# Attention groups with filler: nine score and maximum pairs instead of eight

## The chip, the cores and the metric

The kernel runs on one core of one Trainium2 chip. The metric is the device time of one execution in microseconds (us). The kernel before took a median of 1838.41 us over 3 runs (1837.89 to 1838.9).

The names of the engines are those of the profile: PE is TensorE (PEld its weight loads), DVE is VectorE, ACT is ScalarE, POOL is GpSimd, SP is SyncE.

## What is computed

One transformer block with adaptive normalization, 2048 tokens of width 512, 32 heads of 16, and a gated feed-forward layer of width 1792. Cut to what matters:

```python
mod = silu(c) @ w_mod                                # six vectors sa, ca, ga, sb, cb, gb
h = layernorm(x) * (1 + ca) + sa
q, k, v = (h @ wqkv), cut into 32 heads of 16
p = softmax(q k^T / 4);  o = p v                     # 2048 x 2048 for each head
x = x + ga * (o @ wo)
h = layernorm(x) * (1 + cb) + sb
x = x + gb * ((silu(h @ w_gate) * (h @ w_up)) @ w_down)
```

## The kernel before

**Units and steps.** The queries are cut into 4 chunks of 512, the heads into 8 groups of 4. A chunk and a head group make a unit; there are 32 units. A unit has 16 steps (one for each 128 keys), so there are 512 steps of 4 heads, and 2048 *pairs*. A pair is one score matmul (`score`, L568: keys by queries, whose exponential ACT takes at L570 out of the bank into a tile `pt`, which 13 buffers hold in turn) and one maximum matmul (`max_one`, L521: queries by keys in the other half of the array's rows, whose row maximum DVE takes at L523). The maxima belong to a unit that comes about 20 steps later, whose scores then have their row maximum taken off before the exponential. When a unit's maxima are complete, DVE reduces them (L545), ACT and DVE turn them into rows, and SP sends these to `qop`.

**Value products.** For each step, `pv_step` multiplies the exponentials by the values in two halves of 256 queries (L583: 4 heads side by side in the array's columns, each matmul twice in the trace). One bank, number 7, holds the sum over a unit's 16 steps. After the last step ACT copies the bank to the tile `o` (L587), and the next unit starts in the same bank. `pvs` issues the halves that are due: the first argument bounds their number, and a step may be taken when `4 * step + 8 <= done`, where `done` counts the pairs issued so far.

**Plain and filled stretches.** In a *plain* stretch (`plain`) PE does three pairs, then one or two halves, and so on; scores go round three banks, maxima round four. While the attention of chunk 1, 2 and 3 goes on, the output projection and the feed-forward layer of the chunk before are worked in as *filler*, in *groups* (`filled`): eight pairs with twelve slots of filler between them, then what is queued in `hook` (DVE's work on a finished filler job), then up to six halves, a *burst*. A slot is two matmuls of 64 rows into the banks 3 and 6 (L781). In a group scores go round two banks (4, 5) and maxima round three (0, 1, 2). A tuple says how many slots follow each pair: `TWO` for the output projection and for `gate_up` (24 slots, two groups), `DOWN` for `down` (12 slots, one group). `gate_up` ends with a tanh on ACT (L835) and two DVE operations that empty the banks (L839, L841); `down` ends with two DVE additions (L855), and in its middle ACT reads both banks (L878) before the second six slots may write them.

**What sets the order.** Everything is written out by hand: each engine's queue holds its instructions in the order of the Python calls. A chunk's filler starts at a step of the table `STARTS`: 32 pairs of output projection, plain stretches of `NORM` = 9 and `WIN` = 3 steps, for the last one also `REST` = 24 steps, then the feed-forward jobs, with one plain stretch of 3 steps before the last two `down` jobs. What is left before the next start is plain. `close_unit` sets the steps at which a finished unit's output is scaled and stored, and at which the next chunk's tiles are taken and loaded (`begin`, `load_wo`, `load_o`) and split on POOL (`split_o`). The last 20 steps have no maxima; their groups take eight pairs in five banks.

Of the kernel before, what the change touches and what calls it, by code (L numbers as in the profile page):

```python
# [29 lines left out]
NG = H // 4  # L30
NU = NG * NC
NF = F // P
FG = 2
# [10 lines left out]
PTS = 13  # L44
FBANKS = (3, 6)
KEEP = 7
REST = 24
NORM = 9
STARTS = (147, 275, 403)
TWO = (0, 3, 2, 2, 2, 2, 1, 0)  # L50
DOWN = (0, 3, 3, 0, 3, 3, 0, 0)
ALONE = {TWO: (0, 4, 0, 4, 0, 4, 0, 0), DOWN: (0, 6, 0, 0, 0, 6, 0, 0)}


def run(it):
    for _ in it:
        pass


def take(it, k):  # L60
    run(islice(it, k))
# [40 lines left out]
def block_kernel(ctx, tc, x, wqkv, wo, w_gate, w_up, w_down, c, w_mod, out):  # L102
    nc = tc.nc
# [18 lines left out]
    four, bank, single = Turn(0, 1, 2, 3), Turn(4, 5, 6), Turn(7)  # L122
# [231 lines left out]
    bank = Turn(4, 5, 6, 7)  # L354
# [101 lines left out]
    for ci in range(NC - 1):  # L456
# [6 lines left out]
        if ci == 1:  # L463
            bank = Turn(4, 5, 6)
# [30 lines left out]
    n = 16 * NU  # L495
    last = NC - 1
# [93 lines left out]
    def out_a(u, eng):  # L590
        pv.pop(u)
        o = o_.pop(u)
        dn = pf.tile([P, 16], F32, name="dn", tag="dn", bufs=1)
        eng.dma_start(dn, o[16:P:32, :].rearrange("h (b e) -> h b e", e=16))
        return o, dn
# [17 lines left out]
    def at(i, f):  # L613
        due.setdefault(i, []).append(f)
# [257 lines left out]
    chunks = {}  # L872
# [7 lines left out]
    def begin(ci):  # L880
        x2 = pf.tile([P, 4, D], F32, name="x2", tag="x2", bufs=1)
        act = [pf.tile([P, NK, CW], F32R, name=f"act{a}", tag=f"act{a}", bufs=1) for a in range(2)]
        hT = [pf.tile([P, NK, CW], F32R, name=f"act{a}", tag=f"act{a}", bufs=1) for a in range(2)]
        chunks[ci] = ch = Chunk(ci, x2, act, hT)
        ch.load_x2(nc.sync if ci else nc.gpsimd)
# [18 lines left out]
    four, bank = Turn(0, 1, 2, 3, 6, 7), Turn(4, 5)  # L904
# [4 lines left out]
    def close_unit(u, i):  # L909

        if u == NU - 1:
            res[u] = out_a(u, nc.scalar)
            return
        res[u] = out_a(u, nc.sync)
        if u + 3 < NU:
            load_k(u + 3)
            load_q(u + 3)
        i0 = i if u % NG == NG - 1 else i + 3
        at(i0 + 3, lambda: res.__setitem__(u, out_b(u, nc.sync, *res[u])))
        at(i0 + 4, lambda: res.__setitem__(u, out_r(u, nc.sync, *res[u])))  # L920
        at(i0 + 5, lambda: out_c(u, nc.gpsimd, nc.gpsimd, *res.pop(u)))
        if u % NG == NG - 1:
            if u // NG:
                at(i + 4, lambda: begin(u // NG))
                at(i + 5, lambda: chunks[u // NG].load_wo())
            at(i + 7, lambda: chunks[u // NG].load_o(nc.gpsimd))
            at(i + 9, lambda: chunks[u // NG].split_o())

    at(3, lambda: begin(0))
    at(UG - 2, lambda: chunks[0].load_wo())  # L930
# [26 lines left out]
    halves = [(i, half) for i in range(n) for half in range(2)]  # L957
    done, ended, owed = 0, 0, 0
    three = Turn(0, 1, 2)
# [15 lines left out]
    for i in range(-LEAD, -1):  # L975
# [7 lines left out]
        if i == -2:  # L983
            four, work = three, bank
            for k in range(4):
                bank = Turn(7, 3, 6)
                for _ in range(WIN):
                    pair_of()
                bank = work
# [3 lines left out]
        while side:  # L993
            side.pop(0)()

    def pvs(most, by_halves):

        nonlocal owed
        if by_halves:
            most, owed = most + owed, 0  # L1000
        while most and halves and 4 * halves[0][0] + 8 <= done:
            i, half = halves.pop(0)
            pv_step(i, half)
            most -= 1
            if i % 16 == 15 and half:
                close_unit(i // 16, done // 4 - 1)
                if by_halves:
                    break
        if by_halves and most and halves and 4 * halves[0][0] + 8 <= done:
            owed = most  # L1010
# [18 lines left out]
            pvs((HALVES[(w - 2) % 4] if done > 8 else 0) + (w == 4 * steps // WIN - 1), True)  # L1029
            end_steps()  # L1030

    def filled(places, work):

        nonlocal four, bank, beside
        beside = True
        four, bank = three, Turn(4, 5)
        if done >= 4 * n - 4 * (LEAD - 1):
            places, bank = ALONE.get(places, places), Turn(4, 5, 0, 1, 2)
        for r in range(len(places)):
            pair_of()  # L1040
            take(work, places[r])
            if r % 4 == 3:
                end_steps()
        hook()
        pvs(6, False)

    def two_of(u):
        return [kop[u % 3][:, e, :].rearrange("p (k c) -> p k c", k=NK) for e in range(2)]
# [11 lines left out]
    for ci in range(last):  # L1060
        plain(STARTS[ci] - done // 4)
        ch = chunks[ci]
        for t0 in (0, 2):
            work = out_pair(ch, t0, outs, True)
            filled(TWO, work)
            filled(TWO, work)
        side.append(lambda: scaled(ch))
        plain(NORM)
        plain(WIN, [lambda tp, k=k: ch.turned(tp, k) for k in range(NK)])
        if ci == last - 1:  # L1070
            plain(REST)
        for _ in range(len(ch.jobs) - (KEEP if ci == last - 1 else 0)):
            job, args = ch.jobs.pop(0)
            if args == (NF // FG - 1, 0):
                plain(WIN)
            work = job(ch, *args, outs, True)
            for places in (TWO, TWO) if job is gate_up else (DOWN,):
                filled(places, work)
    chunks[last - 1].load_gu(NF - 2)
    filled((0,) * 4, iter(()))  # L1080


    assert done == 4 * n
# [75 lines left out]
```

## Time and profile before

| what | number |
|---|---|
| median of 3 runs | 1838.41 us |
| the profiled execution | 1838.88 us |
| its span, from first to last instruction | 1837.1 us |
| busy: PE, DVE, ACT, POOL | 99%, 83%, 68%, 25% of the span |
| granted TensorE clock | 1.00 in every stretch |
| plain stretch before the filler of chunk 1: 84 pairs | 885.49 to 936.64 |
| plain stretch before the filler of chunk 2: 84 pairs | 1291.26 to 1342.66 |
| plain stretch `REST`: 96 pairs | 1404.37 to 1463.35 |
| 40 groups of chunk 0's feed-forward jobs: 320 pairs | 592.58 to 864.19 |

The times of the table's last four rows are the starts of the score matmuls with these numbers, counted along the trace. A busy engine is one with an instruction in flight. PE's matmuls overlap in the trace, since they are pipelined; what one costs is read from start to start. The same holds for the exponentials and the maxima: an instruction's duration is longer than the distance to the next one behind it.

### The profile page before, as it was taken

What the parts mean: (1) busy time and instruction counts of PE and PEld (TensorE: products, weight loads), DVE (VectorE), ACT (ScalarE), POOL (GpSimd) and SP (SyncE); (2) the same over time, 40 slices, a digit from 0 to 9 for tenths busy, and PEclk for the clock granted to TensorE, in tenths of its full rate; (3) what the DMA queues carried; (4) which work ended last, traced back from release to release, by engine and by line L of the source; (5) the groups of instructions that cost most, each with busy time, mean ns of one, the idle gap of its engine ahead of it and who ended that gap; (6) DMA issues with size and microseconds to landing.
All of it is one profiled execution on the core that took longest, in us unless ns stands there. A gap on an engine that the chain in (4) does not pass through costs nothing.

```text
span 1837.1 us, 41048 instructions
## 1 busy us (share of the span) xinstructions
PE 1825.5 (99%) x16904; PEld 1198.2 (65%) x16904; DVE 1532.5 (83%) x2578; ACT 1243.7 (68%) x2386; POOL 460.4 (25%) x541
## 2 busy tenths in 40 slices
PE   9999999999999999999999999999999999999999
PEld 7876444444455777776565777776564577777887
DVE  5578999999999888889999888889999988831544
ACT  4223888888877777777878777777878877774211
POOL 3612544565223111111123111111123011130200
PEclk9999999999999999999999999999999999999999
DMA  8884876657845444453544554444643545333642
GB/s 305 286 225 149 183 185 199 168 189 178 209 79 125 102 120 141 118 147 70 149 103 105 134 132 116 123 117 90 158 81 57 111 93 149 138 122 121 271 169 110
DMA packets 80488, 267.63 MB, mean 146 GB/s; under 512 B 19604, under 2 KB 24212, under 8 KB 59620
## 3 DMA queue, kind: packets, MB, share of 16 engines
q1 hardware_dynamic: 61324, 179.71, 33.8%
q0 software_dynamic: 18288, 84.49, 19.3%
q8 instruction: 133, 2.18, 0.5%
q10 hardware_dynamic: 688, 0.80, 0.2%
q14 instruction: 55, 0.45, 0.1%
HBM read 201.85 MB, written 62.13 MB: 144 GB/s over the span
## 4 chain that ended last, share of the span: by engine, by line
PE 96%; DVE 2%; ACT 1%; DMA 1%; SPq 0%; issue 0%; DVEq 0%
PE bank L583 27%; PE bank L781 19%; PE bank L568 18%; PE bank L521 14%; PE bank L791 8%; PE bank L211 7%; DVE mx L523 1%; PE bank L824 1%; DMA wm_ab<-in_w_mod 1%; PE bank L765 0%; DVE stt L807 0%; PE bank L533 0%; PE bank L163 0%; PE bank L534 0%; PE bank L535 0%
## 5 line engine op out<-in xcount | busy, mean ns | idle before, releaser
L523 DVE TENSOR_REDUCE mx<-bank 128x1 f32<-128x512 f32 x2048 | 1276.0, 681 | 108.5 <-PE bank L521 66.2
L568 PE MATMUL bank<-qop,kop 50*128 50x512 f32 x2048 | 730.2, 425 | 1.0 <-ACT pt__16517 L570 0.2
L521 PE MATMUL bank<-kop,qop 48*128 48x512 f32 x2048 | 726.6, 425 | 2.9 <-DVE mx L523 2.6
L568 PEld LDWEIGHTS bank<-qop,kop 50*128 50x128 f32 x2048 | 342.6, 184 | 169.9 <-issue 55.6
L521 PEld LDWEIGHTS bank<-kop,qop 48*128 48x128 f32 x2048 | 343.5, 184 | 113.9 <-DVE mx L523 67.7
L781 PE MATMUL bank<-act,wgu 64*128 64x512 f32 x1872 | 300.9, 392 | 0.0
L781 PEld LDWEIGHTS bank<-act,wgu 64*128 64x128 f32 x1872 | 196.1, 187 | 24.7 <-issue 0.2
L610 POOL TENSOR_TENSOR on<-o,rb 128x512 f32<-128x512 f32 x31 | 39.8, 1284 | 498.1 <-DMA rb<-d_dr 363.6
L781 PE MATMUL bank<-wd,mid 64*128 64x512 f32 x912 | 134.0, 397 | 0.0
L843 POOL CAST mid<-m 128x512 fp32r<-128x512 f32 x40 | 24.3, 608 | 379.3 <-DVE m L841 176.5
L781 PEld LDWEIGHTS bank<-wd,mid 64*128 64x128 f32 x912 | 88.0, 185 | 15.9 <-ACT first L878 3.2
L211 PE MATMUL bank<-hT,wqs 128*128 128x512 f32 x384 | 94.3, 397 | 0.4 <-DVE wqs L351 0.4
L839 DVE SCALAR_TENSOR_TENSOR q<-th,bank 128x512 f32<-128x512 f32 x56 | 38.2, 682 | 54.4 <-ACT th L835 54.4
L211 PEld LDWEIGHTS bank<-hT,wqs 128*128 128x128 f32 x384 | 70.7, 188 | 18.8 <-issue 2.9
L835 ACT ACTIVATE th<-bank 128x512 f32<-128x512 f32 x56 | 33.3, 594 | 58.1 <-PE bank L791 58.1
L855 DVE TENSOR_TENSOR x<-bank,x 128x512 f32<-128x512 f32 x84 | 53.9, 685 | 18.3 <-PE bank L781 16.8
L841 DVE TENSOR_TENSOR m<-bank,q 128x512 f32<-128x512 f32 x56 | 38.7, 691 | 21.7 <-PE bank L791 19.7
L844 POOL TENSOR_TENSOR mid<-m,mid 128x512 fp32r<-128x512 f32 x40 | 51.5, 1287 | 3.3
L791 PE MATMUL bank<-wd,mid 128*128 128x512 f32 x216 | 51.4, 393 | 0.0
L211 PE MATMUL bank<-wqs,hT 128*128 128x512 f32 x192 | 48.0, 398 | 0.0
L781 PE MATMUL bank<-wgu,act 64*128 64x512 f32 x288 | 47.8, 394 | 0.1
L791 PEld LDWEIGHTS bank<-wd,mid 128*128 128x128 f32 x216 | 40.3, 188 | 9.1 <-POOL mid L844 0.3
(6298 smaller groups left out, 5133.0 us busy)
## 6 DMA issues: line engine op xcount, KB each, us to landing
wgu<-gu_dr SPq DMA_DIRECT2D x48, 1024.0 KB
wd<-wd_dr SPq DMA_DIRECT2D x28, 1024.0 KB
kop<-kd SPq DMA_DIRECT2D x33, 768.0 KB
kop<-kd POOLq DMA_DIRECT2D x29, 768.0 KB, 8.8
gu_dr<-wgu POOLq DMA_DIRECT2D x14, 1024.0 KB, 13.5
kd<-prt SPq DMA_DIRECT2D x16, 512.0 KB
qd<-prt SPq DMA_DIRECT2D x16, 512.0 KB
kop<-gu_dr SPq DMA_DIRECT2D x8, 1024.0 KB
```

The lines of the kernel that those rows point to most:

```text
L211: nc.tensor.matmul(pt, lhs(a, k), rhs(b, k), start=(n == 0), stop=(n == 3 * nk - 1))
L521: nc.tensor.matmul(pm, qop[u][rows, s, qt * P:(qt + 1) * P], kop[u % 3][rows, s, kc * CW:(kc + 1) * CW], start=True, stop=True)
L523: nc.vector.tensor_reduce(mx[u][:, b, s, qt, kc:kc + 1], pm, op=ALU.max, axis=AX.X)
L568: nc.tensor.matmul(sp, kop[u % 3][rows, h // 2, kt * P:(kt + 1) * P], qop[u][rows, h // 2, :], start=True, stop=True)
L583: nc.tensor.matmul(pv[u][32 * h:32 * h + 32, cols], v_flat[:, e0:e0 + 32], p_[h][:, cols], start=(kt == 0 and half == 0), stop=(kt == 15), ...
L610: mul.tensor_mul(on, o, rb)
L781: nc.tensor.matmul(outs[e], lhs(e, a, k)[rows], rhs(b, k)[rows], start=(ph == 0 and j == 0), stop=(j == z and (ph == 1 or trade is not None)),
L791: nc.tensor.matmul(outs[e], lhs(e, a, k), rhs(b, k), start=(j == 0), stop=(j == z))
L839: nc.vector.scalar_tensor_tensor(q, th, 1.0, outs[0], op0=ALU.add, op1=ALU.mult)
L841: nc.vector.tensor_mul(m32, outs[1], q)
L844: (nc.gpsimd if slow else nc.vector).tensor_sub(mid[:, 1, :], m32, mid[:, 0, :].bitcast(F32))
L855: nc.vector.tensor_add(ch.x2[:, t, :], outs[e], ch.x2[:, t, :])
```

## The change

A group takes nine pairs for its twelve slots, with new tuples; the groups of eight stay for the output projections of the first two chunks and for the last two `down` jobs of a chunk. As the 2048 pairs are the same, the plain stretches give up what the groups take: the stretches before the filler of chunks 1 and 2 have 48 pairs for 84, and `REST` has 60 for 96. In a filled group a step's value products may start when `4 * step + 5 <= done`, one pair behind the step. The two score banks of the groups now go on in turn from one group to the next. The tiles of the next chunk are taken and loaded some steps later. Every line that this text names by its number stands one line higher in the changed kernel.

```diff
-REST = 24
+REST = 15
-STARTS = (147, 275, 403)
-TWO = (0, 3, 2, 2, 2, 2, 1, 0)
-DOWN = (0, 3, 3, 0, 3, 3, 0, 0)
-ALONE = {TWO: (0, 4, 0, 4, 0, 4, 0, 0), DOWN: (0, 6, 0, 0, 0, 6, 0, 0)}
+STARTS = (147, 276, 405)
+TWO = {9: (0, 3, 1, 2, 1, 2, 1, 2, 0), 8: (0, 3, 2, 2, 2, 2, 1, 0), 0: (0, 4, 0, 4, 0, 4, 0, 0)}
+DOWN = {9: (0, 3, 1, 2, 0, 3, 1, 2, 0), 8: (0, 3, 3, 0, 3, 3, 0, 0), 0: (0, 6, 0, 0, 0, 6, 0, 0)}
...
         if u % NG == NG - 1:
-            if u // NG:
-                at(i + 4, lambda: begin(u // NG))
-                at(i + 5, lambda: chunks[u // NG].load_wo())
-            at(i + 7, lambda: chunks[u // NG].load_o(nc.gpsimd))
-            at(i + 9, lambda: chunks[u // NG].split_o())
+            late_ = 3 if u // NG else 0
+            if late_:
+                at(i + 9, lambda: begin(u // NG))
+                at(i + 9, lambda: chunks[u // NG].load_wo())
+            at(i + 7 + late_, lambda: chunks[u // NG].load_o(nc.gpsimd))
+            at(i + 9 + late_, lambda: chunks[u // NG].split_o())
...
-    def pvs(most, by_halves):
+    def pvs(most, by_halves, lag=8):
...
-        while most and halves and 4 * halves[0][0] + 8 <= done:
+        while most and halves and 4 * halves[0][0] + lag <= done:
...
-    def filled(places, work):
+    two = Turn(4, 5)
+
+    def filled(kind, size, work):
...
-        four, bank = three, Turn(4, 5)
+        four, bank = three, two
         if done >= 4 * n - 4 * (LEAD - 1):
-            places, bank = ALONE.get(places, places), Turn(4, 5, 0, 1, 2)
-        for r in range(len(places)):
+            size, bank = 0, Turn(4, 5, 0, 1, 2)
+        assert done - 4 * (halves[0][0] if halves else 0) + len(kind[size]) <= PTS
+        for k in kind[size]:
             pair_of()
-            take(work, places[r])
-            if r % 4 == 3:
+            take(work, k)
+            if done % 4 == 0:
                 end_steps()
         hook()
-        pvs(6, False)
+        pvs(6, False, 5)
...
             work = out_pair(ch, t0, outs, True)
-            filled(TWO, work)
-            filled(TWO, work)
+            for _ in range(2):
+                filled(TWO, 9 if ci == last - 1 else 8, work)
...
             work = job(ch, *args, outs, True)
-            for places in (TWO, TWO) if job is gate_up else (DOWN,):
-                filled(places, work)
+            for kind in (TWO, TWO) if job is gate_up else (DOWN,):
+                filled(kind, 8 if job is down and args[0] == NF // FG - 1 else 9, work)
```

**Where instructions move, first place: PE in the middle of a `gate_up` group.** bank_63 to bank_65 hold maxima, bank_67 and bank_68 scores, bank_66 and bank_69 filler. Before, from the third pair of such a group:

```order
L521 MATMUL bank_63<-kop_88,qop 128x512
L568 MATMUL bank_67<-qop,kop_1509 128x512 [waits Activation_49]
L781 MATMUL bank_66<-act_1598,wgu 128x512
L781 MATMUL bank_69<-act_1598,wgu 128x512
L781 MATMUL bank_66<-act_1599,wgu 128x512
L781 MATMUL bank_69<-act_1599,wgu 128x512
L521 MATMUL bank_64<-kop_88,qop 128x512 [waits DVE_49]
L568 MATMUL bank_68<-qop,kop_1509 128x512 [waits Activation_49]
```

And in the changed kernel, from the third pair of a group of nine:

```order
L520 MATMUL bank_64<-kop_88,qop 128x512 [waits DVE_49]
L567 MATMUL bank_68<-qop,kop_1509 128x512 [waits Activation_49]
L780 MATMUL bank_69<-act_1598,wgu 128x512
L780 MATMUL bank_66<-act_1598,wgu 128x512
L567 MATMUL bank_67<-qop,kop_1509 128x512 [waits Activation_49]
L520 MATMUL bank_65<-kop_971,qop 128x512 [waits DMASW4_49,DMASW3_49,DVE_49]
L780 MATMUL bank_69<-act_1599,wgu 128x512
L780 MATMUL bank_66<-act_1599,wgu 128x512
L780 MATMUL bank_69<-act_1598,wgu 128x512
L780 MATMUL bank_66<-act_1598,wgu 128x512
L567 MATMUL bank_68<-qop,kop_1509 128x512 [waits Activation_49]
L520 MATMUL bank_63<-kop_971,qop 128x512 [waits DVE_49]
```

Two slots lay between the third and the fourth pair; now there is one, and two between the fourth and the fifth.

**Second place: ACT in a `down` group.** The tiles `pt` are the exponentials, `first` the two small reads in the middle of the job. Before:

```order
L570 ACTIVATE pt__8470<-bank_67 128x512
L570 ACTIVATE pt__8483<-bank_68 128x512
L570 ACTIVATE pt__8496<-bank_67 128x512
L878 COPY first<-bank_66 1x1
L878 COPY first<-bank_69 1x1
L570 ACTIVATE pt__8509<-bank_68 128x512
L570 ACTIVATE pt__8512<-bank_67 128x512
L570 ACTIVATE pt__8523<-bank_68 128x512
L570 ACTIVATE pt__8540<-bank_67 128x512
L570 ACTIVATE pt__8545<-bank_68 128x512
```

Now:

```order
L569 ACTIVATE pt__8624<-bank_68 128x512
L569 ACTIVATE pt__8627<-bank_67 128x512
L569 ACTIVATE pt__8638<-bank_68 128x512
L569 ACTIVATE pt__8647<-bank_67 128x512
L877 COPY first<-bank_66 1x1
L877 COPY first<-bank_69 1x1
L569 ACTIVATE pt__8658<-bank_68 128x512
L569 ACTIVATE pt__8661<-bank_67 128x512
L569 ACTIVATE pt__8672<-bank_68 128x512
L569 ACTIVATE pt__8681<-bank_67 128x512
L569 ACTIVATE pt__8694<-bank_68 128x512
```

The small reads come behind the fourth exponential and not behind the third, and the group ends with five exponentials behind them; the fifth and the sixth pair of the group follow each other without a slot.

**Third place: PE at the end of a unit inside a filled stretch (unit 10).** bank_70 is the bank of the value products (number 7). Before, the last half of the unit's last step, and what follows:

```order
L583 MATMUL bank_70<-pt__7138,v_flat 32x256
L583 MATMUL bank_70<-pt__7156,v_flat 32x256
L583 MATMUL bank_70<-pt__7143,v_flat 32x256
L583 MATMUL bank_70<-pt__7165,v_flat 32x256
L568 MATMUL bank_67<-qop,kop_1509 128x512 [waits Activation_49]
L521 MATMUL bank_63<-kop_88,qop 128x512 [waits DVE_49]
L568 MATMUL bank_68<-qop,kop_1509 128x512 [waits Activation_49]
L521 MATMUL bank_64<-kop_88,qop 128x512 [waits DVE_49]
```

Now:

```order
L567 MATMUL bank_67<-qop,kop_1509 128x512 [waits Activation_49]
L520 MATMUL bank_64<-kop_88,qop 128x512 [waits DVE_49]
L582 MATMUL bank_70<-pt__7109,v_flat 32x256
L582 MATMUL bank_70<-pt__7127,v_flat 32x256
L582 MATMUL bank_70<-pt__7118,v_flat 32x256
L582 MATMUL bank_70<-pt__7138,v_flat 32x256
L582 MATMUL bank_70<-pt__7109,v_flat 32x256
L582 MATMUL bank_70<-pt__7127,v_flat 32x256
L582 MATMUL bank_70<-pt__7118,v_flat 32x256
L582 MATMUL bank_70<-pt__7138,v_flat 32x256
L582 MATMUL bank_70<-pt__7166,v_flat 32x256 [waits Activation_49]
L582 MATMUL bank_70<-pt__7184,v_flat 32x256
```

The burst went from the unit's last step to the next group's pairs; now it goes on with the first step of the next unit, whose first matmul waits for ACT.

More of the change, by code (lines that the diff above doesn't have):

```diff
@@ L1076, in block_kernel @@
             work = job(ch, *args, outs, True)
-            for places in (TWO, TWO) if job is gate_up else (DOWN,):
-                filled(places, work)
+            for kind in (TWO, TWO) if job is gate_up else (DOWN,):
+                filled(kind, 8 if job is down and args[0] == NF // FG - 1 else 9, work)
     chunks[last - 1].load_gu(NF - 2)
-    filled((0,) * 4, iter(()))
+    filled({0: (0,) * (4 * n - done)}, 0, iter(()))
     assert done == 4 * n
```

## The prediction

> **What bounds the kernel now.** I read the page first, then the busy time by windows of the plain and the filled stretches, then the timelines of single groups.
>
> ```profile
> PE 1825.5 (99%) x16904; PEld 1198.2 (65%) x16904; DVE 1532.5 (83%) x2578; ACT 1243.7 (68%) x2386; POOL 460.4 (25%) x541
> PE 96%; DVE 2%; ACT 1%; DMA 1%; SPq 0%; issue 0%; DVEq 0%
> ```
>
> By the page PE is busy for 99% and carries 96% of the chain of waits. But a busy PE may be a waiting one, so the stretches decide (the columns are the length, then busy us of PE, PEld, DVE, ACT, POOL):
>
> ```profile
> 592.58:864.19 271.61, 271.61 (x2885) 200.31 (x2882) 240.19 (x392) 193.85 (x369) 41.79 (x48) 1.00 0.48 119
> 885.49:936.64 51.15, 50.90 (x515) 24.44 (x511) 50.78 (x87) 44.76 (x88) 13.99 (x18) 1.00 0.64 156
> 1404.37:1463.35 58.98, 58.92 (x592) 28.40 (x589) 57.94 (x100) 51.21 (x102) 6.79 (x8) 1.00 0.33 67
> ```
>
> In the plain stretches (second and third row) DVE is busy for 98 to 99%: the row maxima set the pace there. In the 40 filled groups (first row) DVE has 12% to spare and PE sets it. The maxima alone:
>
> ```profile
> 592.58:864.19 271.61, 205.62 (x320) 1.00 0.48 119
> 885.49:936.64 51.15, 50.65 (x85) 1.00 0.64 156
> ```
>
> A plain pair costs between 50.65 / 85 = 0.596 (the maximum alone) and 58.98 / 96 = 0.614 us (all of REST). The last unit ends and stretch ends stay, so I take 0.607.
>
> **A filled group**, `gate_up`, on PE and ACT:
>
> ```profile
> 707.89 0.50 PE L568 MATMUL bank<-qop,kop 50*128 50x512 f32 x1
> 708.23 0.39 PE L568 MATMUL bank<-qop,kop 50*128 50x512 f32 x1
> 709.14 0.42 PE L568 MATMUL bank<-qop,kop 50*128 50x512 f32 x1
> 711.26 0.39 PE L568 MATMUL bank<-qop,kop 50*128 50x512 f32 x1
> 712.43 0.41 PE L568 MATMUL bank<-qop,kop 50*128 50x512 f32 x1
> 712.77 0.40 PE L583 MATMUL bank<-pt__8239,v_flat 128*32 128x256 f32 x1
> 713.01 0.38 PE L583 MATMUL bank<-pt__8239,v_flat 128*32 128x256 f32 x1
> 714.30 0.38 PE L583 MATMUL bank<-pt__8287,v_flat 128*32 128x256 f32 x1
> 714.63 0.50 PE L568 MATMUL bank<-qop,kop 50*128 50x512 f32 x1
> ```
>
> From the second to the eighth pair lie 18 pairs and slots: (712.43 - 708.23) / 18 = 0.233 us each. A value product's record takes (714.30 - 713.01) / 6 = 0.215, a half (two records) 0.43. The first matmul behind a burst is followed 0.34 later, where 0.233 is usual: restarting costs 0.11. The group takes 6.74.
>
> **What the change adds and removes.** By the tuples, 107 groups with maxima take nine pairs: 28 of `gate_up` and 12 of `down` in chunks 0 and 1 each, and 4 of the projection, 17 of `gate_up` and 6 of `down` in chunk 2, before the maxima end. So 77 are of the TWO kind and 30 of the DOWN kind. The filler's slots, the group count and the pairs are the same. The plain stretches give up 36 pairs each.
>
> Removed: 108 x 0.607 = 65.6 us (64.4 to 66.3 by the two ends).
>
> Added, term by term:
>
> 1. Pairs: 107 x 0.233 = 24.9.
>
> 2. Value products. Half as many halves as pairs move: 54 x 0.43 = 23.2. In the plain stretches they cost nothing, for DVE sets the pace; here they are PE's own time. Every fourth burst or so has six halves.
>
> 3. The score banks in a DOWN group. With two banks a pair's score must wait until the exponential two pairs back is done.
>
> ```profile
> 709.62 0.60 ACT L570 ACTIVATE pt__8305<-bank 128x512 f32<-128x512 f32 x1
> 711.69 0.60 ACT L570 ACTIVATE pt__8333<-bank 128x512 f32<-128x512 f32 x1
> 716.37 0.60 ACT L570 ACTIVATE pt__8396<-bank 128x512 f32<-128x512 f32 x1
> 717.03 0.20 ACT L878 COPY first<-bank 1x1 f32<-1x1 f32 x2
> 717.30 0.60 ACT L570 ACTIVATE pt__8409<-bank 128x512 f32<-128x512 f32 x1
> 717.79 0.59 ACT L570 ACTIVATE pt__8416<-bank 128x512 f32<-128x512 f32 x1
> ```
>
> An exponential starts 0.43 (711.26 to 711.69) to 0.48 (709.14 to 709.62) after its score, lasts 0.60, and follows another at 0.49 (717.30 to 717.79). In the new DOWN group, counted from its first pair, the third pair starts at 0.34 + 4 x 0.233 = 1.27, the fourth at 1.74, the fifth at 2.44; the sixth stands right behind the fifth, at 2.67. The third exponential runs from 1.73, so the fourth from 1.73 + 0.49 = 2.22 to 2.82, and the sixth pair starts at about 2.87 by the 0.05 that a release takes in the rows on the bank of the value products below (0.07 there). That is 0.20 late, and 0.11 more for the restart, 0.31 in all. The DOWN groups of today lose something too:
>
> ```profile
> 667.16:673.90 6.74, 3.06 (x8) 1.39 (x8) 1.00 0.02 4
> 714.63:721.48 6.85, 2.83 (x8) 1.39 (x8) 1.00 0.01 2
> 721.48:728.39 6.91, 2.84 (x8) 1.40 (x8) 1.00 0.10 17
> ```
>
> The two `down` groups (second and third row, 8 scores each) last 0.11 and 0.17 longer than `gate_up`; the two small reads of ACT do that, and in the new group they end before the seventh slot is due. So 0.31 - 0.14 = 0.17 each, 30 x 0.17 = 5.1 (0 to 10).
>
> 4. The score banks in a TWO group. The sixth pair is five places of 0.233 behind the fourth, 1.17; the fourth's exponential ends 0.48 + 0.60 + 0.05 = 1.13 behind it. A margin of 0.04: it holds mostly. Where ACT is handed an extra piece (the rows of the maxima, once a unit), it does not. I take 0.02 x 77 = 1.5 (0 to 6).
>
> 5. The bank of the value products. A burst now takes all steps up to 4 x step + 5 = done, and with nine pairs the end of a unit falls inside a burst: unit 10 ends with step 175, and the burst at 713 pairs goes to step 177. Counting on, this happens at 713, 776, 839, 902, 965, 1481, 1544, 1800, 1863 and 1926 pairs: 10 times. The next unit's first product goes into the bank that ACT must still copy out. Before, each unit of the filled stretches ends with its burst, and the copy lies under the next group's pairs. What it costs uncovered is seen in the early plain stretch:
>
> ```profile
> 254.07 0.38 PE L583 MATMUL bank<-pt__2397,v_flat 128*32 128x256 f32 x1
> 254.69 0.61 ACT L587 COPY o<-bank 128x512 f32<-128x512 f32 x1
> 255.37 0.40 PE L583 MATMUL bank<-pt__2425,v_flat 128*32 128x256 f32 x1
> L587 ACT COPY o<-bank x32: 585/587/614, 214.7 to 1676.0; 128x512 f32<-128x512 f32 x32
> ```
>
> From the unit's last record to the next unit's first: 255.37 - 254.07 = 1.30, with pairs between and ACT late with an exponential; the copy ends at 255.30, and PE starts 0.07 later. With ACT idle the copy starts about as an exponential does, 0.45 after the record. So 0.45 + 0.59 + 0.07 = 1.11 where the next record would start after 0.22: 0.89 lost, and PE has nothing else in its queue, behind which the whole group waits. 10 x 0.89 = 8.9 (0 if something covers it, 10.8 if ACT is late as above).
>
> At nothing: DVE in the groups.
>
> ```profile
> 708.46 0.69 DVE L523 TENSOR_REDUCE mx<-bank 128x1 f32<-128x512 f32 x1 [1.52 <-PE bank L568]
> 713.00 0.68 DVE L523 TENSOR_REDUCE mx<-bank 128x1 f32<-128x512 f32 x1
> 713.60 0.68 DVE L839 SCALAR_TENSOR_TENSOR q<-th,bank 128x512 f32<-128x512 f32 x1
> 714.31 0.69 DVE L841 TENSOR_TENSOR m<-bank,q 128x512 f32<-128x512 f32 x1
> ```
>
> The first maximum starts 0.57 into the group (708.46 - 707.89), the next ones 0.6 apart. The ninth pair's bank needs the sixth maximum done, at 0.57 + 5 x 0.607 + 0.69 = 4.30; the pair starts at 0.34 + 19 x 0.233 = 4.77. The two operations that empty the filler's banks follow the ninth maximum (from 5.43): from 6.03 and 6.74 to 7.43, and the next group's first slot is due at 6.97 + 0.34 + 0.23 = 7.54. If these covers of 0.47 and 0.11 went, PE would wait for what exceeds them, in its own queue, and everything behind it. The loads for a chunk's start: they are issued some 24 us ahead of the filler (two plain steps behind the last job, of the 12), before it was 28:
>
> ```profile
> 908.44 1.02 SPq L708 DMA_DIRECT2D wgu<-wo_dr x2
> 930.34 1.29 POOL L730 TENSOR_TENSOR act<-act,act 128x512 fp32r<-128x512 f32 x1
> ```
>
> POOL's last split ended at 931.6, 5 us before the filler at 936.64; without that cover each us late counts at two starts. The table of chunk 0's start, the projection groups of eight and the tail from KEEP on are as before.
>
> Sum: 24.9 + 23.2 + 5.1 + 1.5 + 8.9 = 63.6 added, 65.6 removed: 2.0 us less. The profiled execution (1838.88, span 1837.1) would come to 1836.9; the median lies 0.47 below it, so **1836.4 us**. [...]
>
> **Rivals.**
>
> A. The wait at the unit's end is hidden, or is no wait: 1836.4 - 8.9 = 1827.5; with the DOWN stall at nothing too, 1822. For it: no filled burst of before shows the wait. Against it: the order shows the wait on ACT, and the row at 255.37 shows PE starting as the copy ends. I give 0.27, which also stands for removed pairs being dearer than I take them.
>
> B. Slower: the score banks decide in the TWO groups. If the release comes 0.05 later than I count, the margin of 0.04 is gone, at the sixth and at the eighth pair, and each late score costs 0.11 for the restart as well. At both places, 2 x 0.12 x 77 = 18.5, less the 1.5 counted: 1853; at one, 1844. For it: 0.04 is as small as the spread from 0.43 to 0.48. Against it: ACT's queue is idle behind each second exponential and catches up. 0.15.
>
> C. DVE becomes the bound of the groups. [...] If the ninth pair cost a maximum's 0.607 in place of 0.233: 107 x 0.37 = 40 more, 1876. Against it: the cover of 0.47 above. 0.03.
>
> **Chances.** Forecast 0.55, A 0.27, B 0.15, C 0.03. A measurement of this kernel can tell about 0.2%, 3.7 us, from no change. The forecast's own range is 1831 to 1841; part of it lies under 1834.7. So faster 0.36, same 0.45, slower 0.19. The range takes in A and stops short of B: 1826 to 1843.
>
> **What would show it.** TWO groups of nine at 6.98 us with four halves and 7.84 with six; DOWN groups at 7.28 with their sixth pair 0.2 late behind ACT; ten bursts with a hole of 0.9 before a value product that waits for L587 (L586 then); plain pairs still at 0.61. I am wrong if those holes are missing, if TWO groups take over 7.1, or if a chunk's filler starts late.

## The result: 1862.0 us, slower by 1.2%, and the profile after

The changed kernel takes 1862.01 us in the median of five runs (1852.66 to 1866.43), against 1838.41 before (1837.89 to 1839.11). The ratio is 1.012, with a 95% interval of 1.0103 to 1.0137. The forecast was 1836.4, with a range of 1826 to 1843. The profiled execution took 1864.16 us (span 1862.4), 25.3 more than that of before.

The page of the changed kernel, its busy row of PE and its chain of waits:

```profile
PE 1835.8 (99%) x16886; PEld 1178.6 (63%) x16886; DVE 1514.5 (81%) x2584; ACT 1227.8 (66%) x2383; POOL 460.0 (25%) x541
PE 93%; DVE 2%; DMA 2%; ACT 1%; SPq 0%; issue 0%; DVEq 0%; ACTq 0%
```

PE is still busy for 99%, in a span that is 25 us longer. That row hides the loss. The chain says a little more: DMA went from 1% to 2%, PE from 96% to 93%. The stretches say where (length, then busy us of PE, PEld, DVE, ACT, POOL, then the granted clock): the 40 filled groups of chunk 0, and the three plain stretches.

```profile
592.58:897.23 304.65, 298.90 (x3124) 205.77 (x3121) 257.91 (x436) 208.94 (x410) 43.42 (x50) 0.99 0.44 108
918.64:951.68 33.04, 31.16 (x298) 14.17 (x294) 29.51 (x50) 25.90 (x51) 13.99 (x18) 0.95 0.78 204
1335.03:1370.37 35.34, 32.04 (x299) 14.86 (x295) 29.52 (x50) 25.83 (x51) 13.21 (x18) 0.90 0.86 198
1433.93:1470.79 36.86, 36.60 (x371) 17.57 (x367) 35.91 (x62) 32.26 (x64) 4.88 (x6) 1.00 0.40 64
```

Each plain stretch lost 36 pairs. At 0.607 they should have come to 51.15 - 21.85 = 29.3, 51.40 - 21.85 = 29.6 and 58.98 - 21.85 = 37.1. The last one did. The other two are 3.7 and 5.8 too long, and in these the granted clock is 0.95 and 0.90 where it was 1.00. The 40 groups grew by 304.65 - 271.61 = 33.0; the terms of the forecast give 25.0 for these 40 (pairs 9.3, halves 8.6, DOWN 2.0, TWO 0.6, five unit ends 4.5). So there are two places to look at, inside the groups and at the chunks' starts. What PE waited for (us in total, times, longest):

```profile
PE bank L582 <- ACT o L586: 7.1, 10, 0.8
PE bank L567 <- DMA qop<-mr: 4.8, 2, 3.1
PE bank L520 <- DVE mx L522: 3.0, 6, 0.9
PE bank L780 <- DMA wgu<-gu_dr: 2.2, 1, 2.2
```

The first row is the forecast's wait at ten unit ends. The second and the fourth are transfers, and the forecast has neither.

**Inside the groups.** Four single groups by windows: TWO with six halves, TWO with four, DOWN with four, and a TWO group with six in which a unit ends.

```profile
743.42:751.36 7.94, 7.94 (x94) 5.52 (x91) 5.64 (x10) 4.94 (x9) 0.00 (x0) 1.00 0.93 287
765.61:772.74 7.13, 7.13 (x79) 5.20 (x75) 6.53 (x13) 5.43 (x11) 1.38 (x2) 1.00 0.10 37
691.26:698.59 7.33, 7.33 (x79) 5.19 (x76) 6.73 (x11) 5.04 (x11) 0.00 (x0) 1.00 0.81 117
837.35:846.20 8.85, 8.14 (x94) 5.42 (x90) 5.69 (x10) 5.53 (x10) 1.15 (x2) 1.00 0.94 303
```

Forecast were 7.84, 6.98, 7.28 and 7.84 + 0.89 = 8.73. The DOWN group and the unit's end came out. The TWO groups are 0.10 to 0.15 too long, and the busy row can't show it: it reads 7.94 of 7.94 and 7.13 of 7.13 us, because a matmul that waits inside its record counts as busy (below, a score's record of 0.47 us where 0.39 is usual). The timeline of one such group (PE, PE's weight loads, ACT) does:

```profile
1053.12 0.50 PE L567 MATMUL bank<-qop,kop 50*128 50x512 f32 x1
1054.21 0.59 ACT L569 ACTIVATE pt__12567<-bank 128x512 f32<-128x512 f32 x1
1054.86 0.18 PEld L567 LDWEIGHTS bank<-qop,kop 50*128 50x128 f32 x1 [0.19 <-ACT pt__12567 L569]
1054.88 0.47 PE L567 MATMUL bank<-qop,kop 50*128 50x512 f32 x1
1055.19 0.63 PE L780 MATMUL bank<-act,wgu 64*128 64x512 f32 x4
1055.66 0.39 PE L567 MATMUL bank<-qop,kop 50*128 50x512 f32 x1
1056.04 0.18 PEld L567 LDWEIGHTS bank<-qop,kop 50*128 50x128 f32 x1
1057.24 0.18 PEld L567 LDWEIGHTS bank<-qop,kop 50*128 50x128 f32 x1 [0.21 <-ACT pt__12601 L569]
1057.96 0.18 PEld L567 LDWEIGHTS bank<-qop,kop 50*128 50x128 f32 x1 [0.18 <-ACT pt__12610 L569]
1058.06 0.40 PE L567 MATMUL bank<-qop,kop 50*128 50x512 f32 x1
```

The second exponential ends at 1054.80. The fourth score needs its bank. What waits is not the score but the load of its weights: it starts 0.06 after the exponential's end, lasts 0.18, and the score's record is 0.47 long where 0.39 is usual. The filler's next slot starts at 1055.19, 0.39 behind the exponential's end. With the forecast's release of 0.05 and a place of 0.233 it would be 0.28. So a release costs 0.16 here, not 0.05. It is not one late score: in at least 71 of 76 TWO groups of nine in the trace, the weight load of each score from the third to the ninth starts within 0.08 of the end of the exponential two pairs back. From one load to the next on the same bank it takes 1.18 to 1.22 in the group shown (1054.86, 1056.04, 1057.24 for the fourth, sixth and eighth score, 1056.74 and 1057.96 for the seventh and ninth), where five places are 1.17, and this adds up: the ninth score starts 1058.06 - 1053.12 = 4.94 behind the first, where 0.34 + 19 x 0.233 = 4.77 was forecast.

**At a chunk's start.** SP's and POOL's queues of the changed kernel, and behind them two pieces of its chain of waits:

```profile
920.52 1.28 POOL L609 TENSOR_TENSOR on<-o,rb 128x512 f32<-128x512 f32 x1 [8.80 <-DMA rb<-d_dr]
922.90 1.08 POOL L856 DMA_DIRECT2D out<-x  x2 [0.23 <-DVE mx L522]
926.58 0.39 SPq L702 DMA_DIRECT2D x<-in_A_x  x1
927.02 1.77 SPq L707 DMA_DIRECT2D wgu<-wo_dr  x2
933.07 1.13 SPq L538 DMA_DIRECT2D qop<-mr  x2
...
933.67 5.79 DMA qop<-mr
1346.21 8.86 DMA qop<-mr
```

The same queue before:

```profile
908.00 0.39 SPq L703 DMA_DIRECT2D x<-in_A_x  x1
923.14 1.13 SPq L539 DMA_DIRECT2D qop<-mr  x2
```

The rows of the maxima are 2 x 8 KB. Before, they were issued 15.1 us behind the loads of x (1 MB) and of wo (2 x 1 MB), and no wait for them shows. Now it is 6.5 us, they take 5.79 (8.86 at the next start), and the next unit's scores stand still. The load of x (issued at 926.58) waits in SP's queue for x's tile, and two stores of that tile (922.90) stand in POOL's queue behind the normalisation `on`, which waits for `rb`. Before, the stores were issued at 884.31.

**Behind a wait the clock falls.** Stretches of the changed kernel around the wait for `wgu<-gu_dr`, behind the first wait for `qop<-mr`, and in the normalisation of chunk 1 (26.09 us, 24.30 before):

```profile
803.00:807.00 4.00, 1.79 (x22) 0.88 (x16) 2.30 (x4) 1.09 (x2) 1.86 (x2) 1.00 0.87 343
807.00:811.00 4.00, 4.00 (x24) 3.64 (x23) 2.08 (x3) 1.79 (x3) 0.00 (x0) 0.57 0.04 16
940.00:945.00 5.00, 5.00 (x42) 2.10 (x44) 3.04 (x5) 2.67 (x6) 0.00 (x0) 0.66 0.96 147
986.00:988.00 2.00, 1.11 (x13) 0.39 (x11) 1.90 (x8) 1.25 (x3) 0.39 (x2) 1.00 0.03 4
988.00:996.00 8.00, 8.00 (x54) 3.49 (x54) 6.22 (x11) 4.12 (x9) 6.55 (x18) 0.57 0.45 147
```

In slices of 1 us the clock of this trace is 1.00 or 0.50, with one value between at an edge (0.76, 0.50, 0.50, 0.54 and 1.00 from 807 on). So a mean of 0.57 over 4 us is 4 x 0.43 / 0.5 = 3.4 us at half. The 0.66 over 5 us gives 3.4 too, the 0.57 over 8 us 6.9. Behind each wait PE calls itself busy throughout. The trace's clock record has two more such dips: 6.8 us from 1353.64, in the middle of the second wait for `qop<-mr`, and 3.4 us from 561.75, ahead of the groups, where no listed wait of PE is over 0.3 us. The five dips make 23.9 us at half clock. If PE sets the pace all the while, that is an estimated 11.9 us lost.

The mean granted clock of each run suggests that such dips make the spread of the five runs as well. It is 1.000 for the run of 1852.66 us, then 0.998 (1857.73), 0.996 (1862.01), 0.994 (1864.16) and 0.993 (1866.43). With (1 - clock) times the span taken off, an estimate good to about 1 us, the five runs come to 1852.7 to 1854.6, 2 us apart in place of 14.

### The profile page after: what moved, and what is told of

The parts are those of the page before. It is cut to its first block, busy times and chain, and to the rows that moved or that the text cites. A ratio compares the mean times of both kernels' runs of the same rounds, so it can differ in the third digit from the quotient of the medians.

```text
span 1862.4 us, 41110 instructions
## 1 busy us (share of the span) xinstructions
PE 1835.8 (99%) x16886; PEld 1178.6 (63%) x16886; DVE 1514.5 (81%) x2584; ACT 1227.8 (66%) x2383; POOL 460.0 (25%) x541
## 4 chain that ended last, share of the span: by engine, by line
PE 93%; DVE 2%; DMA 2%; ACT 1%; SPq 0%; issue 0%; DVEq 0%; ACTq 0%
PE bank L582 26%; PE bank L780 19%; PE bank L567 17%; PE bank L520 15%; PE bank L790 8%; PE bank L210 7%; DVE mx L522 1%; DMA wgu<-gu_dr 1%; DMA qop<-mr 1%; PE bank L823 1%; DMA wm_ab<-in_w_mod 0%; PE bank L764 0%; DVE stt L806 0%; ACT o L586 0%; PE bank L162 0%
## 5 line engine op out<-in xcount | busy, mean ns | idle before, releaser
L522 DVE TENSOR_REDUCE mx<-bank 128x1 f32<-128x512 f32 x2048 | 1259.9, 680 | 152.9 <-PE bank L520 89.9
L567 PE MATMUL bank<-qop,kop 50*128 50x512 f32 x2048 | 767.0, 434 | 5.8 <-DMA qop<-mr 4.8
L520 PE MATMUL bank<-kop,qop 48*128 48x512 f32 x2048 | 751.5, 430 | 3.2 <-DVE mx L522 3.0
L567 PEld LDWEIGHTS bank<-qop,kop 50*128 50x128 f32 x2048 | 346.5, 185 | 200.9 <-issue 36.9
L520 PEld LDWEIGHTS bank<-kop,qop 48*128 48x128 f32 x2048 | 347.2, 186 | 126.8 <-DVE mx L522 61.6
L780 PE MATMUL bank<-act,wgu 64*128 64x512 f32 x1872 | 315.1, 394 | 2.2 <-DMA wgu<-gu_dr 2.2
L780 PE MATMUL bank<-wd,mid 64*128 64x512 f32 x912 | 148.5, 396 | 0.0
L780 PEld LDWEIGHTS bank<-wd,mid 64*128 64x128 f32 x912 | 94.8, 186 | 12.9 <-ACT first L877 1.6
## 6 DMA issues: line engine op xcount, KB each, us to landing
kop<-kd POOLq DMA_DIRECT2D x29, 768.0 KB, 10.6
```

The source lines that it names most:

```text
L520: nc.tensor.matmul(pm, qop[u][rows, s, qt * P:(qt + 1) * P], kop[u % 3][rows, s, kc * CW:(kc + 1) * CW], start=True, stop=True)
L522: nc.vector.tensor_reduce(mx[u][:, b, s, qt, kc:kc + 1], pm, op=ALU.max, axis=AX.X)
L567: nc.tensor.matmul(sp, kop[u % 3][rows, h // 2, kt * P:(kt + 1) * P], qop[u][rows, h // 2, :], start=True, stop=True)
L780: nc.tensor.matmul(outs[e], lhs(e, a, k)[rows], rhs(b, k)[rows], start=(ph == 0 and j == 0), stop=(j == z and (ph == 1 or trade is not None)),
```

## The experiments

Two theories for the groups: the score banks (the price of a release), or something common to all groups. Two for the starts: the order of the transfers, or the late table of loads by itself. The runs go in that order; every time is a median, each ratio is to runs of before on the same chip.

**x4_half: the price of the release.** The exponential runs over the first 256 queries only, and both halves of the value products read that half; the other 256 queries' exponentials are left out.

```diff
-        nc.scalar.activation(p_, sp, AF.Exp, scale=SCALE)
+        nc.scalar.activation(p_[:, 0:HQ], sp[:, 0:HQ], AF.Exp, scale=SCALE)
...
-  ... v_flat[:, e0:e0 + 32], p_[h][:, cols],
+  ... v_flat[:, e0:e0 + 32], p_[h][:, 0:HQ],
```

> The changed kernel, but ACT takes the exponential of the first 256 queries of a pair only, and both halves of the value products use it: the exponentials of the other 256 queries are left out. [...] Theory W: in the groups of nine a score's weight load waits for the exponential two pairs back, and only then starts its 0.19 us, so that release costs about 0.16 and not 0.05 us, and the five places of 1.17 us between two scores are not enough. With short exponentials the TWO groups of nine with four halves should fall from 7.11 to 6.98 us, the DOWN groups from 7.32 to 7.0, and the holes at the unit ends stay. Rival: nine pairs with single slots between them are slower on PE by themselves (the turns between the halves of the array), and the TWO groups stay at 7.11.

Measured: 1846.29 us (1841.2 to 1849.66), ratio 1.0036 (1.0025 to 1.0047), 15.7 less than the changed kernel. A TWO group and a DOWN group by windows, and in the TWO group the second exponential and the fourth score with its weights:

```profile
1047.50:1054.47 6.97, 6.97 (x79) 4.99 (x76) 6.37 (x11) 3.84 (x10) 0.00 (x0) 1.00 1.05 185
1061.53:1068.67 7.14, 7.14 (x78) 4.84 (x74) 6.80 (x13) 3.46 (x11) 0.00 (x0) 1.00 0.25 64
...
1048.37 0.38 ACT L569 ACTIVATE pt__12567<-bank 128x256 f32<-128x256 f32 x1
1049.00 0.19 PEld L567 LDWEIGHTS bank<-qop,kop 50*128 50x128 f32 x1
1049.23 0.40 PE L567 MATMUL bank<-qop,kop 50*128 50x512 f32 x1
```

The exponential lasts 0.38 where it was 0.59 and ends at 1048.75; the weights are loaded 0.25 behind it and ahead of the score, which again lasts 0.40. TWO falls from 7.13 to 6.97, DOWN from 7.33 to 7.14. That is the forecast's price of a pair without a release, so the score banks make the difference: (7.13 - 6.97) x 77 = 12 us in TWO groups and (7.33 - 7.14) x 30 = 6 in DOWN groups. The medians over all the groups of the two traces say nearly the same: TWO groups fall from 7.12 to 6.98 with four halves and from 7.98 to 7.85 with six, which is 0.14 x 57 + 0.13 x 20 = 10.6 us, and DOWN groups with four from 7.32 to 7.13. In x4 only 3 to 5 of the 76 TWO groups still have a weight load within 0.08 of an exponential's end at the fifth to the ninth score, and none at the fourth. The waits at the unit ends (7.1) are as they were. The fall of the median holds dips as well: these runs have a clock of 0.992 to 0.996, those of the changed kernel 0.993 to 1.000.

**x1_loads and x2_units: the two transfers, one at a time.** x1 moves the loads of x and wo behind the rows of the maxima in SP's queue; x2 lets a unit's close issue the loads of kop and qop two steps later, behind the next weights.

```diff
-                at(i + 9, lambda: begin(u // NG))
-                at(i + 9, lambda: chunks[u // NG].load_wo())
+                at(i + 9, lambda: begin(u // NG, False))
+                at(i + 12, lambda: chunks[u // NG].load_x2(nc.sync))
+                at(i + 12, lambda: chunks[u // NG].load_wo())
...
```

```diff
-            load_k(u + 3)
-            load_q(u + 3)
+            at(i + 2, lambda: load_k(u + 3))
+            at(i + 2, lambda: load_q(u + 3))
```

> The changed kernel, with the loads of a chunk's input rows and projection weights issued three steps later (step i + 12 in place of i + 9), which puts them behind the maxima's transfer to qop in SP's queue. Theory D (transfers): the stretches of 48 pairs lost 3.6 and 5.9 us (33.04 and 35.34 where 48 pairs at 0.61 take 29.4), because that transfer of a few KB came behind 3 MB of loads and PE stood and then ran at a lower granted clock. So both stretches should take 29.4 to 30 us and the kernel 1851 to 1854. Rival P (the pattern of pairs and bursts itself costs it): the stretches stay at 33 to 35 and the time at 1862.

> The changed kernel, with the loads of the keys and queries three units ahead issued two steps after a unit's end and not at it. Theory D: one gate_up group of chunk 0 took 11.87 us because its weights landed 2.2 us late behind those loads, and the granted clock fell to 0.59 behind the wait. So the weights should go ahead of the loads, no group should wait for them, and the kernel should be 3 to 6 us faster than the changed one (1856 to 1859). Rival: the loads collide two steps later with the next weights, and the time stays at 1862 or rises.

Measured: x1 1858.44 (1856.56 to 1858.94), ratio 1.0107 (1.0092 to 1.0122); x2 1858.09 (1856.37 to 1860.89), 1.0108 (1.0091 to 1.0125). x2 came out as expected; x1 missed its 1851 to 1854. In x1 the wait for `qop<-mr` is gone, the plain stretches fall to 29.63 and 29.77, as the forecast had them, and the wait for `wgu<-gu_dr` is 0.8 in place of 2.2. But wo, loaded last, is now late itself, from the waits of x1:

```profile
PE bank L780 <- DMA wgu<-wo_dr: 4.1, 1, 4.1
```

In x2 the wait for `wgu<-gu_dr` is gone, that for `qop<-mr` stays (4.2), and 10.2 us at half clock follow the first one.

**x3_both: x1 and x2 together.**

> Both moves of loads together. Theory D: no transfer is waited for any more, 1846 to 1850, and the runs spread by less than the 14 us of the changed kernel (1852.66 to 1866.43). What is left above 1838.4 (8 to 11 us) is then the pattern's own: the TWO groups at 7.11 for a forecast of 6.98, the unit ends inside a burst, the DOWN groups at 7.32. Rival P: above 1855.

Measured: 1855.44 (1854.09 to 1858.54), ratio 1.0095 (1.008 to 1.011). The expectation missed: wo is waited for as in x1 (4.2, once), and the first group of the projection takes 13.45 us where 6.80 is usual. The lateness only changed its bearer.

**x5_clean: no transfer waited for.** x3, and wo loaded at step i + 5 into buffers that are free by then; only x stays at i + 12.

```diff
+                at(i + 5, lambda: wo_early(u // NG))
...
+                at(i + 12, lambda: chunks[u // NG].load_x2(nc.sync))
```

> The version with both moves of loads, and now the projection weights of the next chunk are loaded at step i + 5 (their buffers are free by then), only the input rows at i + 12. In the version before, one projection group still waited 4.2 us for these weights and lasted 13.45 us. Theory D: that group falls to 6.8 us, no transfer is waited for, 1846 to 1849. The 8 to 10 us above 1838.4 are then the pattern's own: 107 groups of nine that cost more on PE than the plain pairs they replace. Rival: another transfer becomes late in its place, and the time stays above 1852.

Measured: 1848.52 (1848.21 to 1850.81), ratio 1.0054 (1.0039 to 1.0069), as expected. The 40 groups of chunk 0 and the plain stretches by windows:

```profile
593.92:894.60 300.68, 297.15 (x3124) 204.04 (x3120) 257.11 (x436) 208.75 (x410) 43.35 (x50) 1.00 0.44 110
916.03:945.63 29.60, 29.41 (x298) 13.96 (x294) 29.07 (x50) 25.66 (x51) 13.86 (x18) 1.00 0.76 190
1326.81:1356.60 29.79, 29.59 (x298) 14.28 (x295) 29.17 (x50) 25.66 (x51) 13.63 (x18) 1.00 0.81 186
1420.23:1457.10 36.87, 36.60 (x370) 17.56 (x367) 35.92 (x62) 32.26 (x64) 4.88 (x6) 1.00 0.40 64
```

The clock is 1.00 throughout these stretches, and PE waits for no transfer from the attention on. So 1862.01 - 1848.52 = 13.5 us of the changed kernel come with the late transfers and with stretches at half clock. One of these, in the normalisation of chunk 1, follows a wait for DVE. The other 10.1 are the pattern of nine itself; they are 8.8 by the median of before on the chip of x5 (1839.75).

**x7_before_late: the late table alone.** The kernel before, with eight pairs, with later steps for begin and load_wo as in the changed kernel, and load_o and split_o two steps later (there three).

```diff
-                at(i + 4, lambda: begin(u // NG))
-                at(i + 5, lambda: chunks[u // NG].load_wo())
+                at(i + 9, lambda: begin(u // NG))
+                at(i + 9, lambda: chunks[u // NG].load_wo())
...
```

> The kernel before with its groups of eight, and only the table of loads changed: the next chunk's input rows and projection weights at step i + 9 (i + 4 and i + 5 before), the attention's result at i + 9, split at i + 11. Theory D: the late table alone brings the wait for the maxima's transfer: the stretches of 84 pairs take 53 to 57 us in place of 51.2 and 51.4, and the kernel 1842 to 1849. Rival: without groups of nine the transfers keep out of each other's way, and it stays at 1838.

Measured: 1838.33 (1837.48 to 1840.53), ratio 0.9995 (0.9986 to 1.0004): the time of before, and the expectation missed. SP's queue of this run:

```profile
909.88 0.39 SPq L703 DMA_DIRECT2D x<-in_A_x  x1
924.90 1.13 SPq L539 DMA_DIRECT2D qop<-mr  x2
```

Still 15.0 us apart. The step in the table sets only the order in SP's queue; the load goes out when the queue reaches it and the tile is free, and here nothing in between holds it. So the table is not the cause; when x's tile comes free may be.

**x9_stores and x10_stores_units: the tile set free earlier.** The stores of finished rows go through SP's queue, not POOL's; x10 adds the edit of x2.

```diff
-                    (nc.sync if ch.ci == last else nc.gpsimd).dma_start(od[:, 4 * ch.ci + t, :], ch.x2[:, t, :])
+                    nc.sync.dma_start(od[:, 4 * ch.ci + t, :], ch.x2[:, t, :])
```

> The changed kernel, with one thing altered: the stores of a chunk's finished rows (out<-x) go through SP's queue in chunks 0 and 1 too, not through POOL's. Theory P: the rows of the maxima (qop<-mr) come late because the loads of x and of wo start only at 926.6, 6.5 us ahead of them, and those start late because x's tile is held by two stores that stand in POOL's queue behind the normalisation of the last unit (on, which waits for rb until 920.5). By it the stores are now issued right behind rb (about 915.5), the load of x at 919 to 920 (a store takes some 3.9 to land), 13 us ahead of the maxima's rows; no wait for qop<-mr, plain stretches 29.6 to 30.2 instead of 33.0 and 35.3, about 8 to 9 us less in all: 1851 to 1855. The wait for wgu<-gu_dr and the dip of the clock behind it may stay. Rival Q: the transfers collide because of the shorter stretch alone, whoever stores: the wait for qop<-mr stays above 3 us in sum and the time above 1858.

> The kernel before this one in the list (stores of out<-x through SP), and in addition the loads of the next unit's kop and qop two steps later in SP's queue than the unit's close. Theory P with the loads of the weights behind the unit's loads: no transfer is waited for in the filled part, 1847.5 to 1851, as with the loads put in another order by hand (1848.5). Rival Q: the wait for qop<-mr stays, 1854 to 1859.

Measured: x9 1861.16 (1859.04 to 1863.37), ratio 1.012 (1.0103 to 1.0137); x10 1855.39 (1851.34 to 1858.7), 1.009 (1.0073 to 1.0108). Both expectations missed on the time. SP's queue of x9 at the two starts, then its piece of the chain at the second:

```profile
919.28 0.93 SPq L856 DMA_DIRECT2D out<-x  x2
922.89 0.39 SPq L702 DMA_DIRECT2D x<-in_A_x  x1
935.17 1.12 SPq L538 DMA_DIRECT2D qop<-mr  x2
...
1335.28 0.39 SPq L702 DMA_DIRECT2D x<-in_A_x  x1
1344.57 1.12 SPq L538 DMA_DIRECT2D qop<-mr  x2
...
1345.15 7.83 DMA qop<-mr
```

At the first start the distance grows from 6.5 to 12.3 us, the wait is gone and the stretch takes 29.82. At the second it grows from 5.8 to 9.3 only; the rows still take 7.83 and the stretch 34.81. x10 shows the same pair: 12.5 apart, no wait, 29.61; 9.3 apart, 7.47 for the rows, 33.06. The mechanism holds start by start, but at the second the loads still went out too late. In x10 the clock counts as well: with its runs' 0.995 to 0.999 taken off as above, they come to 1848.6 to 1851.1, about the expected 1847.5 to 1851. In x9 the wait for `wgu<-gu_dr` (2.5) and the slow normalisation of chunk 1 (26.23) stayed as well, so the median hardly moves.

**x6_split: the unit ends.** x5, and where a unit ends inside a burst, the rest of the burst is issued behind the second pair of the next group and the slots that follow it.

```diff
+                if cut:
+                    left = sum(4 * k + lag <= done for k, _ in halves[:most])
+                    break
...
```

> As x5, and where a unit ends inside a burst, the rest of the burst is issued behind the second pair of the next group and its three slots. Theory U (unit ends): ten holes of 0.7 us go, ten more changes between pairs and value products of 0.2 to 0.35 us come: 3.5 to 5 us faster than x5, 1841 to 1845. Rival: the holes were cover for something else (the exponentials catch up in them), and the time falls by less than 1.5 us.

Measured: 1846.97 (1844.05 to 1849.99), ratio 1.004 (1.0026 to 1.0053). The wait on L586 is gone from the list, and the 40 groups of chunk 0 go from 300.68 to:

```profile
591.99:890.24 298.25, 298.06 (x3125) 203.83 (x3121) 256.92 (x436) 208.24 (x410) 43.34 (x50) 1.00 0.43 110
```

So five unit ends give 2.4 us, 0.49 each, of the 0.7 that each waited; that the rest goes into the second start of a burst is argued, not shown. The median fell by only 1.5, which misses the expected 3.5 to 5, and its spread overlaps x5's. With the clocks of the runs taken off as above (0.997 to 1.000 in both), x6 comes to 1842.5 to 1844.4 and x5 to 1846.7 to 1849.0. By this estimate the edit is worth 4.5 us, ten times 0.45, and the half-clock stretches hide it.

**x8_all: x6 with the half exponential of x4** (again 256 of 512 queries' exponentials left out).

> As x6, and ACT takes the exponential of the first 256 queries of a pair only, whose result both halves of the value products use: the exponentials of the other 256 queries are left out. Late transfers, unit ends and late score banks are then all gone, and only the first terms of the forecast are left: 65.6 us of plain pairs removed, 24.9 + 23.2 us of pairs and value products added. Those terms alone give 1838.4 - 17.5 = 1821; with the restarts of ten split bursts 1821 to 1826. If it stays above 1830, the first terms are wrong, and nine pairs cost PE more than their parts.

Measured: 1828.84 (1828.31 to 1829.22), ratio 0.9943 (0.9926 to 0.996). It lies between what was expected and the point from which the first terms would be wrong. TWO groups take 6.97, DOWN groups 7.06 to 7.13. The normalisation of chunk 1 takes 26.36 here too, 2.5 more than in x5, with the clock at 0.87 over it; without that 2.5 us the time would be 1826.3, at the upper end of the expected range.

No kernel that computes everything beats the one before: the best with nine pairs is x6, 0.4% slower.

## Why the prediction was wrong, point by point

The sign of the forecast was wrong. 2.0 us less were forecast and 23.6 more came.

- **Removed, 65.6 us: right.** With no transfer late (x5) the three stretches give up 51.15 - 29.60, 51.40 - 29.79 and 58.98 - 36.87, 65.3 in all.
- **Terms 1 and 2 (pairs and halves): right as far as they can be seen apart.** x4's TWO group of 6.97 is 6.74 + 0.233. Two more halves cost 7.94 - 7.13 = 0.81, so 0.41 for one, forecast 0.43.
- **Term 3 (DOWN groups): right**, 7.33 by the row above against 7.28.
- **Term 5 (unit ends): right.** Ten waits, as counted. The list gives PE's idle time alone (7.1 us); the group with a unit's end is 8.85 - 7.94 = 0.91 longer, forecast 0.89.
- **Term 4 (score banks in TWO groups) was mis-sized**: 1.5 us forecast, 10.6 (by the medians) to 12.3 (by the groups shown) measured. The step that failed is the sentence that takes the release as 0.05 "in the rows on the bank of the value products". On that bank it holds: behind the ten waits of the changed kernel the value product starts 0.05 to 0.06 after the end of ACT's copy. It nearly holds for the start of the score's record as well (1054.88, 0.08 behind the exponential's end), but the record then carries the score's own weight load of 0.18, and the place behind it comes 0.11 later than 0.05 would have it. From one load to the next on a bank it takes 1.18 to 1.22, not 1.13, so the margin of 0.04 is gone at every pair from the fourth on. Rival B named this mechanism, with two places (the sixth and eighth pair) where the trace has all of them; its 8 to 17 us hold the 9 to 11 that were missing. I gave it 0.15 because ACT's queue was free to catch up. It does, and that does not matter, since the delay lies behind the exponential, not ahead of it. In the traces of the changed kernel and x4 the wait for ACT at the two score banks makes 0.13 to 0.16 us for each TWO group.
- **The loads "at nothing" were wrong, and were off by more than any term.** The filler did start on time: the loads went out 951.68 - 926.58 = 25.1 us ahead of it, 24 forecast, and POOL's cover held. What was missed is the other transfer in that queue, the rows of the maxima. I costed the moved loads by when the filler needs them and did not ask what stands behind them on SP. Row for row: 33.04 - 29.60 and 35.34 - 29.79, 9.0 us at two starts; the wait for `wgu<-gu_dr` and its dip, 304.65 - 300.68 = 4.0. That is 13.0. The normalisation of chunk 1, 26.09 - 23.85 = 2.2, is a dip behind a wait for DVE and not the loads' own. Together 15.2, where the medians of the changed kernel and x5 differ by 13.5. No term of the forecast had a clock below 1.00 either.
- **The sum redone**: -2.0 forecast, and 9.1 to 10.8 for term 4 (10.6 to 12.3 less the 1.5 counted), is +7.1 to +8.8; x5 measures 10.1 by its median. With 13.5 for the transfers and the dips that is 20.6 to 22.3 of the 23.6. The rest has no row of its own.
- **Rival A** (unit ends hidden) did not happen; even x6 recovers only part. **Rival C** did not happen: DVE went from 83% to 81%, its wait on L520 from 2.6 to 3.0.
- **Range and chances**: the range stopped short of B and left the transfers no room above 0; slower at 0.19 was too low. The prediction's own signs of error ("TWO groups take over 7.1") came true. Its other sign, a late start of the filler, was the wrong one to watch.

## What to carry to other kernels

When a group is packed to within a few hundredths of a microsecond of a buffer's release, price the release up to the next instruction's start, with the weight load that waits, from a row in which that instruction itself waited (0.16 us here, where 0.05 was taken). When a change shortens a stretch, list everything in each queue between the moved load and its user, small transfers first, and keep big loads well ahead of an 8 KB transfer that someone waits for (12 us were enough for 3 MB here, 9.3 were not). Read the granted clock behind each new wait, because what follows a short wait can cost more than the wait: behind the one of 0.9 us stood 6.8 us at half clock, and the normalisation took 26.09 us, where x5 with the same wait at full clock took 23.85.

## What the hardware showed that was not expected

- **Half the clock for 3.4 us or twice that followed short waits.** Dips of 3.4, 3.4 and 6.8 us followed waits of 2.2, 1.7 and 0.9 us, and one of 6.8 us began inside the wait of 3.1 us. The 0.9 us wait in the normalisation of chunk 1 is there in x5 too, where the clock stays full:

```profile
980.00:982.00 2.00, 1.11 (x12) 0.45 (x12) 1.90 (x8) 1.25 (x3) 0.42 (x3) 1.00 0.04 7
982.00:990.00 8.00, 7.89 (x74) 3.60 (x74) 8.00 (x14) 6.37 (x14) 6.53 (x18) 1.00 0.44 148
```

  What differs is the moment. The dips of the changed kernel start at 561.75, 807.51, 940.63, 988.42 and 1353.64, which are 72, 39, 14 and 107 times 3.413 us from one to the next, and the trace's clock record gives 3.413 us for the three shorter dips and 6.827 for the two longer ones. So all of them start and end on one grid of 3.413 us. The same 0.9 us wait stands in all ten traces with nine pairs. Counted from the last point of its trace's grid, it begins at 0.17, 0.77, 1.07, 3.18 and 3.25 us in the five traces in which a dip follows (x8, x9, the changed kernel, x2, x4), and at 1.24, 1.48, 1.93, 2.88 and 2.95 in the five in which none does (x10, x6, x3, x5, x1). So the ten traces part by the wait's place on the grid, a pattern found after the fact. What else it takes for a dip is not shown: in x4 a wait of 1.4 us, at 1259.54, is followed by none.
- **8 KB took 5.8 to 8.9 us to arrive** when issued 5.8 to 9.3 us behind 3 MB of loads of the same queue; 12 us behind them nobody waited for it. Other queues were at work too (POOL's moved 2.7 MB from 920 to 945), but with the 3 MB alone moved behind it (x1) the wait was gone.
- **A step in the table of loads is a place in a queue, not a time**: x7 moved two loads by five and four steps, and their distance to the next transfer went from 15.1 to 15.0 us.
